# One-core attention and maxout kernel: another written order of the work, the engine of every eviction in that order, another head

## The chip, the cores and the metric

The kernel runs on one core of a Trainium2 chip. The core has a matmul engine (TensorE, PE in the profile, with its weight loads shown as PEld), three engines that calculate on rows of 128 partitions (VectorE is DVE, ScalarE is ACT, GpSimd is POOL), and a queue engine (SyncE, SP). Matmuls write to PSUM, which has eight banks of 128 x 512 numbers in float32; DVE and ACT read the banks and write to SBUF (an eviction). Each engine does its instructions in the order in which the program lists them, and waits where an operand is not there yet. The metric is the device time of one execution in microseconds, median of several runs.

## The reference

The kernel computes two stages one after the other. The first is attention through 32 inducing vectors: `h` is a softmax-weighted mean of each batch's rows of x, and each row of x then takes a softmax-weighted mean of the 32 rows of `h`. The second is a maxout network on each of the 4 x 12544 rows.

```python
x: (4, 12544, 128) float32;  inducing: (32, 128);  w1, w2: (128, 1024);  w_out: (1024, 128)

def mab(q, kv):
    s = scale * (q @ kv.transpose(0, 2, 1))      # scale = 1/sqrt(128)
    s = s - s.max(-1, keepdims=True)
    a = np.exp(s)
    a /= a.sum(-1, keepdims=True) + 1e-09
    return a @ kv
h = mab(I, x)                # I: inducing for each batch; h: (4, 32, 128)
y = mab(x, h)                # (4, 12544, 128)

g = np.maximum(y @ w1, y @ w2)
out = g @ w_out              # (50176, 128) float32
```

## The kernel before, in words

**What it calculates.** max(a, b) is a + relu(b - a), so the network is a linear part through w1 @ w_out and a part relu(y @ (w2 - w1)) @ w_out. With e = exp(scale * x @ h^T), of 32 numbers for each row, y @ (w2 - w1) is e @ (h @ (w2 - w1)) over the sum of e. The relu is taken before the division, which is positive, and the division comes last. The small matrix h @ (w2 - w1) is `hwd`, (32 x 1024), and h @ w1 @ w_out is `m1`, (32 x 128). Both are held four times over, on partitions 0-31, 32-63, 64-95 and 96-127 (quarters q = 0 to 3), so that four matmuls with 32 rows of weights run side by side on PE.

**The pieces.** A batch has 98 chunks of 128 rows. Blocks (28 in all) hold up to four chunks in each of four quarters. One **unit** is 128 x 512 numbers of relu input: four (or two, or one) matmuls with K = 32 into one PSUM bank, then one eviction with relu to SBUF in float16, on ACT (L1102) or DVE (L1105). There are 784 of them. The **final** matmuls (`final_one`, L932, 3136 of them, 128 x 128 x 128) multiply the relus by w_out and accumulate a **group** of up to four chunks in another bank; the linear part is added there by K = 32 matmuls with `m1`; `evict_group` (L964 on DVE, L971 on ACT) multiplies by one over the sum of e and stores 256 KB to DRAM from SP (L989).

**The order by hand.** PE's whole stream is written out in a string `ORDER` of words. A number is that many finals. `pN` is a phase (`phase`, L1031): up to N units of different quarters at once, in PE's row mode (32 x 128 tiles); a quarter that is left out with N below 4 may carry the linear part of a group. `s` is `stage` (L643-670): x @ h^T for a block in column mode (128 x 32 tiles), then exp on ACT. `c`, `t`, `a`, `r`, `e`, `h`, `w`, `m` make the next batch's h: scores (L356), a DMA transpose of their exponentials (`pool_turn`, L395), their product with x (`pool_accum`, L414), and the small steps from it. `xB.J` is a DMA transpose of part J of batch B's x (`transpose_x_dma`, L208) and `gK` the transpose of block K's e (`turn_e2`, L711), after which POOL adds it up and takes reciprocals. Both go to SP's queue, between the stores. PE has three modes in this list: row (`p`), column (`s`, `c`, `a`), and full (the rest). I call a run of words of one mode a segment.

**The planner.** While the list is read, an object `Clock` adds up times of its own for each engine. Its times choose the PSUM bank of each step, and, before the change, the engine of each relu eviction: in `phase` the engine that would be done first takes it, and a number after the point (`p4.13` is 1101 in binary) flips single choices. A string `EVICT` has one digit for each group: 0 for DVE, 1 for ACT.

**The head.** Batch 0 has no h yet. Its x comes in parts of 14 chunks or fewer (`parts[0]`, twelve of them). The first is loaded by SP as float32 and cast by DVE and ACT (L784, L785); the others are loaded by POOL's queue (`load_x`, L195), and the DMA casts from float32 to float16 on the way. The string `HEAD` orders PE there: `3a 3b` transposes the two halves of part 3 on PE (`p1_transpose`, L276; half a is evicted by DVE at L280, half b by ACT at L283), `S3` makes its scores (`p1_scores`, L292) and the exp on ACT (L305), `A3` accumulates h and the sums (`p1_accum`, L319 and L328). Then come the weights: w1 and w2 loaded as float32 by POOL's queue, their difference, the transposes of w1 (`weights_2`, `weights_2b`, L589, L596, L599) and the product w1 @ w_out (`weights_3`, L607, the word `W`). `H` is `second_half`: the second half of `hwd` and the second half of the transposes of w1.

## Time and profile before

| quantity | value |
|---|---|
| time, median of 3 runs | 317.69 us (317.68 to 318.22) |
| the profiled execution's own time | 317.76 us |
| its span in the profile | 316.0 us |
| mean granted clock of PE | 0.998 |
| PE busy | 308.6 us (98%) |
| ACT busy / DVE busy / POOL busy | 280.2 (89%) / 274.5 (87%) / 125.8 us (40%) |
| relu evictions on ACT / on DVE | 470 / 314 |
| mean DMA traffic | 177 GB/s |

The span is what the profiler saw from the first instruction to the last; the execution's own time is 1.76 us more. The page's first part has the busy time of each engine. A matmul's record is longer than the step from it to the next one, since matmuls are pipelined (219 ns on the record of a final, 56 ns from one to the next in the trace), so the busy share of PE does not say how near PE is to its peak. What PE's stream costs is read from the starts of its matmuls. The word list and the trace can be laid side by side: the trace has 151 stretches of row-mode matmuls after the head, and the list has 151 row segments.

### The profile page before, as it was taken

What the parts mean: (1) busy time and instruction counts of PE and PEld (TensorE: products, weight loads), DVE (VectorE), ACT (ScalarE), POOL (GpSimd) and SP (SyncE); (2) the same over time, 40 slices, a digit from 0 to 9 for tenths busy, and PEclk for the clock granted to TensorE, in tenths of its full rate; (3) what the DMA queues carried; (4) which work ended last, traced back from release to release, by engine and by line L of the source; (5) the groups of instructions that cost most, each with busy time, mean ns of one, the idle gap of its engine ahead of it and who ended that gap; (6) DMA issues with size and microseconds to landing.
All of it is one profiled execution on the core that took longest, in us unless ns stands there. A gap on an engine that the chain in (4) does not pass through costs nothing.

```text
span 316.0 us, 12577 instructions
## 1 busy us (share of the span) xinstructions
PE 308.6 (98%) x5308; PEld 239.9 (76%) x5308; DVE 274.5 (87%) x488; ACT 280.2 (89%) x580; POOL 125.8 (40%) x187
## 2 busy tenths in 40 slices
...
GB/s 203 208 252 205 207 219 146 207 229 230 127 218 245 245 183 174 190 233 207 121 225 252 213 227 215 204 174 203 106 85 118 100 106 118 119 88 140 102 120 101
DMA packets 81336, 55.81 MB, mean 177 GB/s; under 512 B 62816, under 2 KB 66176, under 8 KB 81280
## 3 DMA queue, kind: packets, MB, share of 16 engines
...
q0 software_dynamic: 5968, 13.70, 22.4%
...
q14 instruction: 15, 0.12, 0.1%
HBM read 27.28 MB, written 25.69 MB: 168 GB/s over the span
## 4 chain that ended last, share of the span: by engine, by line
PE 94%; DMA 2%; ACT 1%; DVE 1%; issue 1%; POOL 0%; POOLq 0%
PE ps L932 60%; PE ps L1085 23%; DMA xn<-in_x_dram 2%; PE ps L657 2%; PE ps L356 2%; PE ps L414 2%; PE ps L276 1%; PE ps L328 1%; PE ps L292 1%; PE ps L521 0%; DVE relu L1105 0%; PE ps L319 0%; ACT e L669 0%; DVE o L964 0%; ACT e_first L696 0%
## 5 line engine op out<-in xcount | busy, mean ns | idle before, releaser
L1102 ACT ACTIVATE relu<-ps 128x512 f16<-128x512 f32 x470 | 241.0, 627 | 17.5 <-PE ps L1085 16.5
L1105 DVE TENSOR_SCALAR relu<-ps 128x512 f16<-128x512 f32 x314 | 199.7, 684 | 20.6 <-PE ps L1085 19.0
L932 PE MATMUL ps<-woutp,relu 128*128 128x128 f16 x3136 | 203.5, 219 | 0.2
L932 PEld LDWEIGHTS <-relu 128*128 128x128 f16 x3136 | 176.6, 98 | 34.4 <-issue 28.7
L1085 PE MATMUL ps<-e,hwd 32*128 32x512 f16 (+2 forms) x840 | 82.8, 361 | 0.1
L720 POOL TENSOR_TENSOR half<-ed 128x256 f32<-128x256 f16 (+2 forms) x23 | 14.1, 613 | 145.8 <-DMA ed<-e 145.8
L724 POOL TENSOR_TENSOR rd<-den,minus 128x16 f32<-128x16 f32 (+2 forms) x23 | 60.7, 2639 | 1.8
L964 DVE TENSOR_TENSOR o<-ps,rd 128x512 f32<-128x512 f32 (+3 forms) x83 | 53.2, 643 | 3.9 <-PE ps L1085 2.8
L1085 PE MATMUL ps<-m,e 32*128 32x128 f16 x372 | 36.8, 216 | 0.0
L1085 PEld LDWEIGHTS <-hwd 32*128 32x128 f16 x880 | 26.7, 91 | 12.8 <-issue 3.8
L1085 PEld LDWEIGHTS <-e 32*128 32x128 f16 x372 | 22.4, 92 | 10.4 <-issue 2.7
L720 POOL TENSOR_TENSOR half<-half 128x32 f32<-128x32 f32 (+3 forms) x69 | 22.3, 323 | 5.4
L195 POOL DMA_DIRECT2D xn<-in_x_dram x32 | 17.6, 563 | 5.7 <-DMA xn<-in_x_dram 4.3
L280 DVE COPY xT<-ps 128x512 f16<-128x512 f16 (+3 forms) x12 | 5.7, 485 | 8.6 <-PE ps L276 8.6
L964 DVE TENSOR_TENSOR o<-ps,rp 128x512 f32<-128x512 f32 (+3 forms) x20 | 12.8, 642 | 0.0
L369 ACT ACTIVATE eu<-ps 128x512 f16<-128x512 f32 x18 | 11.0, 617 | 0.6 <-PE ps L356 0.3
L669 ACT ACTIVATE e<-ps 128x512 f16<-128x512 f32 (+2 forms) x21 | 11.1, 607 | 0.3 <-PE ps L657 0.2
L283 ACT COPY xT<-ps 128x768 f16<-128x768 f16 (+3 forms) x10 | 5.7, 574 | 4.3 <-PE ps L276 4.2
L276 PE MATMUL ps<-identity,xn 128*128 128x128 f16 x98 | 7.6, 220 | 1.4 <-DMA xn<-in_x_dram 0.9
L657 PE MATMUL ps<-xT,hT 128*32 128x512 f16 (+3 forms) x110 | 8.1, 361 | 0.1
L276 PEld LDWEIGHTS <-xn 128*128 128x128 f16 x98 | 5.5, 97 | 2.9 <-DMA xn<-in_x_dram 1.2
L356 PE MATMUL ps<-xT,inducingT 128*32 128x512 f16 x72 | 6.8, 386 | 0.0
...
## 6 DMA issues: line engine op xcount, KB each, us to landing
...
xT<-xn SPq DMA_TRANSPOSE x33, 4.4
...
```

Of the source, the lines that this page charges most:

```text
L195: nc.gpsimd.dma_start(out=xn_at[b, i][:, 0:n, :], in_=xr[b, :, k0 : k0 + n, :])
L276: nc.tensor.transpose(ps[:, j, :], xn[:, g + j, :], identity16)
L356: nc.tensor.matmul(out=ps[32 * g : 32 * (g + 1), :], lhsT=inducingT, rhs=xT_tiles[b % 2][:, U * u + 4 * g : U * u + 4 * (g + 1), :], start ...
L657: nc.tensor.matmul(out=ps[32 * q : 32 * (q + 1), 128 * t : 128 * (t + n)], lhsT=hq, rhs=xT[:, c : c + n, :], start=True, stop=True, tile_p ...
L669: nc.scalar.activation(out=blk.e2[:, 0 : 128 * wd], in_=ps[:, 0 : 128 * wd], func=AF.Exp, scale=st[0]["rs"] if blk.b == 0 else scale,)
L720: nc.gpsimd.tensor_tensor(out=dst, in0=cur[:, :, 0:n], in1=cur[:, :, n : 2 * n], op=ALU.add)
L724: nc.gpsimd.tensor_tensor(out=rp[:, 0:wd, :].rearrange("p t q -> p (t q)"), in0=den[:, 0 : 4 * wd], in1=minus1[:, 0 : 4 * wd], op=ALU.pow,)
L932: nc.tensor.matmul(out=g.ps[:, 128 * c : 128 * (c + 1)], lhsT=g.blk.relu[g.q][:, 128 * (jb * w4 + t) : 128 * (jb * w4 + t + 1)], rhs=woutp ...
L964: nc.vector.tensor_mul(osb[:, 0:m, :], g.ps[:, 0 : m * C].rearrange("p (s c) -> p s c", s=m), g.blk.rp[:, t0 : t0 + m, q : q + 1].broadcas ...
L1085: nc.tensor.matmul(**seq.pop(0))
L1102: nc.scalar.activation(out=dst, in_=src, func=AF.Relu)
L1105: nc.vector.tensor_scalar(out=dst, in0=src, scalar1=0.0, scalar2=None, op0=ALU.max)
```

## The change

- **Head.** Batch 0 is cut into thirteen parts instead of twelve. Six of them (2 to 7, 56 chunks) are now loaded by POOL's queue as float32 without a cast, into slots of the relu buffers that are still free (`homes`, `wide`). A word `C` in `HEAD` (`cast_x`) then casts one of them: the first half on DVE, the second half on POOL, after which POOL issues the next load. Eight loads are issued at the start and the others one after each cast, or at the word `L`. `x` after a transpose word swaps its eviction between DVE and ACT. The sums of the exponentials are padded to four chunks, and the two parts of two chunks share one. The three small operations on the identity (`diag`, `rep32`, `repd`) are ahead of the first cast on DVE. The second difference of the weights is on POOL instead of DVE, the second cast of w1 on POOL instead of ACT, and all eight transposes of w1 are in one word `V` after `H`.
- **List.** `ORDER` is another list, with the same 3136 finals, 27 stages, 18 scores and 33 transposes of x. The number after the point of a `p` is now the engine of each eviction itself (bit set: DVE). `EVICT` has six groups on ACT instead of five, the last three among them. The words `x` stand elsewhere, behind the times that the planner has for the landing of their loads.
- **Buffers and planner.** PSUM is one tile with eight slices, the relu buffers and the output buffers are fixed slices of tiles instead of buffers of a pool; their number is the same. The planner's constants are others. A way to split a final in four (`narrow`) is in the code, and no word of the list uses it.

```diff
-    PAIR = 0.0558
-    SWITCH = {"full": 0.11, "row": 0.097, "col": 0.097}
+    PAIR = 0.0563
+    SWITCH = {
+        "full": {"row": 0.095, "col": 0.095},
+        "row": {"full": 0.082, "col": 0.088},
+        "col": {"full": 0.1, "row": 0.094},
+    }
...
+    psall = psum.tile([128, 8, 512], F32, name="psall", tag="psall")
+    relus = [big.tile([128, 2, 4096], F16, name=f"relus{q}", tag=f"relus{q}") for q in range(4)]
...
-    parts[0] = [(0, 14), (14, 14), (28, 14), (42, 14), (56, 7), (63, 7), (70, 7), (77, 7), (84, 6), (90, 4), (94, 2), (96, 2)]
+    parts[0] = [(0, 14), (14, 7), (21, 7), (28, 14), (42, 14), (56, 7), (63, 7), (70, 7), (77, 7), (84, 6), (90, 4)]
+    parts[0] += [(94, 2), (96, 2)]
...
+        homes = {0: (2, 0, 0, 14), 2: (0, 1, 0, 7), 3: (1, 1, 0, 14), 4: (2, 1, 0, 14)}
+        homes.update({5: (0, 1, 7, 7), 6: (3, 1, 0, 7), 7: (3, 1, 7, 7)})
...
+        def load_next():
+            dst, src = later.pop(0)
+            nc.gpsimd.dma_start(out=dst, in_=src)
+
+        load_next()
+        make_identity(nc, identity16)
+        load_next()
+        make_identity(nc, identity32)
+        for _ in range(6):
+            load_next()
...
+        def cut(n):
+            h = min(8, (n + 2) // 2)
+            return (0, h), (h, n - h)
+
+        def cast_x(i):
+
+            for half, (g, m) in enumerate(cut(parts[0][i][1])):
+                eng = nc.gpsimd if half else nc.vector
+                eng.tensor_copy(out=xn_at[0, i][:, g : g + m, :], in_=wide[i][:, g : g + m, :])
...
+            load_next()
...
         HEAD = """
-        1a 1b I S0 2a 2b S1 A0 S2 3a 3b A1 4a 4b S3 S4 A2 A3 5a 5b A4 6a 6b S5 7a 7b S6 A5 8a 8b S7
-        A6 9a 9b 10a S8 11a N S9 S10 A7 S11 A8 A9 A10 A11
+        1a 1b 0b C2 I 2b 2a S0 C3 S1 C4 S2 A0 A2 C5 3b A1 3ax 4a 4b S3 5b C6 5a 6a S4 C7 A3 S5 6b A4 L
+        7ax 7bx S6 A5 8bx 8a 9a 9b S7 A6 10bx 10a 11ax S9 12a N S8 S10 A7 S11 S12 A9 A8 A10 A11 A12
         """
...
-        for i in range(7):
-            if i == 3:
-                difference(nc.gpsimd, 512, J, 22.4, 1.2)
+        load_x(1, 0)
+        difference(nc.vector, 0, 256, 20.45, 0.34)
+        difference(nc.gpsimd, 256, 512, 20.45, 0.64)
+        load_x(1, 1)
+        load_x(1, 2)
+        difference(nc.gpsimd, 512, J, 22.35, 1.25)
+        cast_w1(1)
+        for i in range(3, 7):
             load_x(1, i)
-        difference(nc.vector, 0, 256, 21.0, 0.3)
         sums = small_h(0)
-        difference(nc.vector, 256, 512, 21.0, 0.3)
-        weights_2(0)
...
-                if (max(ck.act, ready) + 0.477 <= max(ck.dve, ready) + 0.597) != bool(flip >> k & 1):
-                    nc.scalar.activation(out=dst, in_=src, func=AF.Relu)
...
+                relu_out(q, blk, unit, bi, ready, bool(vector >> k & 1))
...
         ORDER = """
-        s p4.13 s H1 W g2 p4.1 p2 8 m0 4 p3 p2.1 10 p3 p2 13 p3.2 6 p4.5 22 p2 p4.8 17 x1.0 p4.8 4 g1 11
-        p4.1 13 p4.9 p1 16 p3.4 p2 14 p4.10 6 x1.1 4 x1.2 x1.3 x1.4 x1.5 x1.6 2 p3.6 s s s s 6 g3 6 p4.5
-        14 x1.7 1 x1.8 p4.8 19 p4.10 p2.1 12 x1.9 5 p3 14 p4.4 c1.0 15 p1 p4.5 14 p4.3 g4 13 p4.8 25 p4.6
-        p3.2 10 x1.10 17 p2 p3.1 15 c1.1 p4.2 12 t1.1 2 p3 6 p4.2 4 g5 11 c1.2 c1.3 p4.1 18 p4.4 t1.3 21
-        p3.5 p3 22 c1.4 p1.1 p4.1 19 p2 p4.8 5 g6 21 p4.2 p2 c1.5 19 r1 a1.1 p3.2 p4 t1.5 19 a1.3 p4.9
-        p2.2 29 p3.3 p4 26 p4.1 a1.5 5 p3.1 p2.3 1 e1 11 p4.12 1 h1 17 w1 s s s s p3.2 19 m1 15 p4.6 p3.6
-        30 p3.1 p3.3 24 p3 p3.3 27 p3.2 p3.1 20 p4.3 p2 15 s p4.1 18 p2.1 p3 15 g7 g8 7 p3.3 p4.2 9 g9 12
-        x2.0 3 x2.1 x2.2 s p1.1 p4.4 x2.3 12 p4.5 14 p4.6 14 p4 14 p3 21 p3.6 p4.8 14 g10 4 x2.4 4 x2.5
-        x2.6 9 p4.13 s c2.0 14 p4.6 p1 5 x2.7 4 x2.8 13 p3.3 p3.4 23 p4.4 11 c2.1 p4 p1 9 t2.1 4 g11 x2.9
-        4 x2.10 10 p4.3 p3 15 c2.2 p3.3 21 p3.1 p3.5 27 p3.3 p3.2 c2.3 19 p4.10 4 g12 4 t2.3 5 p4.1 17
-        p3.1 p3.4 16 a2.1 c2.4 p3.1 p3.1 23 p4.4 18 p2.1 p4.9 13 g13 17 p4.9 p3.3 24 a2.3 c2.5 p4.1 p2 7
-        t2.5 12 r2 18 p3 p4.2 30 p4.10 p2.2 16 a2.5 p4.3 p3.6 8 e2 10 p4.2 2 h2 21 p3.1 p3.6 11 w2 4 m2
-        15 p4.11 s s s 13 p3 p2 12 s p4 15 p2 p3.2 22 p3.5 p3.2 3 x3.0 4 x3.1 19 p3.4 p4.12 25 p3.3 13 p3
-        p3.3 27 p3.2 p3.5 12 g15 8 g14 3 p4 11 s s p3.1 p2.2 14 x3.2 4 x3.3 4 x3.4 x3.5 5 p3.1 p4.5 19
-        x3.6 17 p3.4 p4.1 23 g16 14 p4.4 p3 27 c3.0 s p3.1 15 x3.7 c3.1 p4.2 p1 x3.8 15 p4.4 21 p3.4 p3 8
-        g17 14 p3.3 p2 6 t3.1 12 p4.2 p1 20 p3.4 p3.4 22 p4.10 p2.1 30 p4.3 p3 4 g18 8 x3.9 4 x3.10 7
-        c3.2 a3.1 c3.3 p4.3 p2 9 t3.3 15 p4.4 17 p2.1 p4.8 27 p2.2 p4.1 13 g19 18 p3.3 p4.4 10 r3 8 c3.4
-        c3.5 a3.3 p4.5 20 t3.5 1 p4.8 p2.2 21 p4.4 13 p3.5 p2 1 g20 27 p4.4 p3.3 27 a3.5 p4.8 p2.3 2 e3
-        16 h3 14 p3.5 p4.2 10 w3 4 m3 15 s p4.1 9 g21 10 p3.1 p2.1 15 p3.5 s s s 13 p3.1 p3.4 22 p4.8 p1
-        27 p4.3 p3 9 g22 13 p2.2 p2 22 p3.2 p4.3 25 s s p3.4 13 p3 p3.3 30 p4.9 p3.2 g23 21 p4.2 20 p4.1
-        p2.2 30 p3.4 p4.2 24 s p2 p3.2 12 p4.8 g24 22 p4.6 p2.2 20 p2.1 p3.2 16 p3.1 p2 11 p4.9 21 p4.3 9
-        p1 p3 g25 p1 20 p3.1 p3.4 30 p4.8 p3.1 26 p4.8 13 p4.6 13 p4.3 9 g26 13 p3.3 p3 27 p3.5 p2 22 p2
-        p4.1 22 p2.2 p4.9 22 p3 p2.1 g27 27 p4.1 p3.2 38 p4.3 p3.1 31 p2 p4.9 22 p2.1 p3.1 24 p3 p4.11 40
-        p3.4 p3 21 p4.6 21 p2.1 p3.4 31 p4.4 p4.3 63
+        s p3.2 p3.3 s H1 V W p3.4 p3.4 8 m0 5 g2 3 p3.2 4 p3.4 9 p3.6 7 p4.2 12 p3.1 10 p4.5 8 p3.2 10
+        p4.4 x1.0 21 p4.3 p1 10 p4.10 x1.1 23 p2.1 p4.1 23 x1.2 x1.3 p3.2 9 p4.13 s s s 18 p1 p4.5 x1.4
+        14 p4.1 4 g3 13 p4.12 9 p3.1 3 x1.5 8 p4.12 15 c1.0 x1.6 p3.3 p2 16 p4.1 10 x1.7 6 x1.8 5 p4.3
+        p2.1 14 s c1.1 p3.4 6 x1.9 g4 8 p4.9 15 p4.6 8 p3.4 20 p2.1 p4.1 22 p4.10 11 p1 p4.12 3 x1.10 14
+        c1.2 c1.3 p4.9 21 g5 p4.1 t1.1 p2.1 t1.3 27 p4.12 p2 21 p4.10 20 p4.12 p2 23 p4.12 a1.1 c1.4 a1.3
+        c1.5 p3.2 11 r1 t1.5 14 p4.12 p3.1 31 p3.4 g6 p3.1 10 a1.5 p4.2 4 e1 16 h1 6 p4.9 p3.4 18 w1 9 s
+        s p4.9 25 p3.1 p3.4 33 p4.12 p3 23 m1 3 p3.4 16 p2.2 p4.4 20 p1.1 p3.1 16 p4.9 8 s s p3.2 2 x2.0
+        14 p2.2 p4.4 21 p4.5 22 p3.2 g9 p3.4 9 x2.1 14 x2.2 p4.12 6 x2.3 13 x2.4 p4.8 p2.1 5 x2.5 23 p2.2
+        p4.8 23 x2.6 x2.7 p2.1 p3.4 12 p4.4 16 p4.12 11 p3.5 g10 c2.0 c2.1 15 x2.8 p1 p4.12 14 p4.8 17
+        p4.6 13 p3.6 s x2.9 t2.1 s c2.2 15 p4.5 10 p3.2 p2.2 x2.10 14 g11 p4.4 15 p4.3 15 c2.3 p2.3 p4 27
+        p2.2 p4.2 31 p4.1 p3.3 28 p4.3 t2.3 10 g12 c2.4 g8 a2.1 c2.5 p3.2 p3.2 28 p2.1 t2.5 p4.8 23 p4.12
+        10 s a2.3 p2.2 p4.4 28 p4.8 p2.2 1 g13 r2 13 a2.5 p3.4 5 p4.2 8 e2 6 p4.8 24 p3.2 p3.1 10 h2 20
+        p4.8 p2.1 12 w2 5 m2 6 p3.5 s s s 10 p4.9 22 p4.12 p2.1 18 p4.1 15 p3.4 13 p3.2 6 p4.5 7 x3.0 7
+        p4.12 9 s p3.6 21 p4.8 p2.2 19 g15 12 x3.1 x3.2 p4.1 p3.1 30 p2.2 p4.8 31 x3.3 p3 p4.12 29 p4.10
+        11 p3.1 g16 12 c3.0 p4.12 18 x3.4 x3.5 3 p4.2 p3.4 4 x3.6 26 p3.6 p3 20 p3.7 x3.7 s x3.8 s c3.1
+        12 p4.1 14 g17 t3.1 p4.12 21 p3.2 p4.10 19 x3.9 7 p2.1 p3.4 24 p3.4 p3.4 23 p4.12 x3.10 18 p2.1
+        g18 p4.8 14 p3.5 c3.2 a3.1 s c3.3 13 p3.4 p3.2 23 p4.10 6 p3.2 12 g1 p4.12 t3.3 21 p2.2 p4.2 7 r3
+        27 g19 p3.1 p4.6 28 p4.6 c3.4 a3.3 c3.5 10 p4.5 p2 12 t3.5 21 p3.2 p4.12 31 p3.4 p3.2 23 g20 g7
+        p4.2 a3.5 p1 p3.4 11 e3 2 p4.2 12 h3 11 p3.4 p3.5 7 w3 8 s s s p3.2 8 m3 13 p1 g21 p4.1 23 p3.6
+        p2 16 p4.8 15 p3.3 8 p4.2 27 p3.3 p4.2 23 p3.4 17 g22 6 p4.10 p3.1 39 p3.6 p3 31 p3.1 p4.5 31
+        p2.2 p4.2 11 g23 p3.2 17 p4.5 15 p4.14 s s s 20 p3.2 p3.4 26 s p4.3 12 p3.4 6 g24 p4.2 22 p2.1
+        p4.8 21 p4.12 12 p1 p4.5 14 p4.6 21 p2 p4.9 20 g25 5 p3.2 3 p4.6 17 p4.3 19 p4.8 p2.2 31 p3.6
+        p4.8 g14 31 p2.1 p4.3 12 g26 p3.2 21 p2.1 p4.4 32 p4.7 p3 32 p2 p4.6 32 p3.4 p4.3 31 g27 p2.1
+        p4.2 28 p4.1 p2.1 24 p4.1 p2.1 31 p3.2 p3.6 28 p2 p4.12 25 p2 p3.1 36 p3.1 p4.1 51
         """
 
-        EVICT = "000000000000000000000000101000000000000000000000010000000000000000000010000000000000000000000000000000010000"
+        EVICT = "000000000000000000000000000000000000000000000000000100000000000000000000000001000000000000000000000010000111"
```

293 lines of the change are left out of this document (168 added, 125 removed).

## The prediction

> **What bounds the kernel now.** I read the page first: its busy shares, the costliest groups and the chain that ended last.
>
> ```profile
> span 316.0 us, 12577 instructions
> PE 308.6 (98%) x5308; PEld 239.9 (76%) x5308; DVE 274.5 (87%) x488; ACT 280.2 (89%) x580; POOL 125.8 (40%) x187
> PE 94%; DMA 2%; ACT 1%; DVE 1%; issue 1%; POOL 0%; POOLq 0%
> L1102 ACT ACTIVATE relu<-ps 128x512 f16<-128x512 f32 x470 | 241.0, 627 | 17.5 <-PE ps L1085 16.5
> L1105 DVE TENSOR_SCALAR relu<-ps 128x512 f16<-128x512 f32 x314 | 199.7, 684 | 20.6 <-PE ps L1085 19.0
> L932 PE MATMUL ps<-woutp,relu 128*128 128x128 f16 x3136 | 203.5, 219 | 0.2
> L1085 PE MATMUL ps<-e,hwd 32*128 32x512 f16 (+2 forms) x840 | 82.8, 361 | 0.1
> ```
>
> The chain is PE for 94% of the span, and PE's two great groups have 0.2 and 0.1 us of idle time before them, while both evicting engines lose some 17 to 21 us waiting for PE. So PE's own stream is the time, from about 30 us on. The busy times by stretch and the chain's start say where that is not so.
>
> ```profile
> 0.00:23.00 23.00, 20.00 (x352) 15.26 (x353) 9.81 (x32) 12.46 (x27) 12.50 (x29) 1.00 1.03 222
> 23.00:31.00 8.00, 6.72 (x107) 4.58 (x106) 7.16 (x16) 7.44 (x17) 3.36 (x5) 1.00 1.06 203
> 31.00:97.00 66.00, 66.00 (x1136) 50.17 (x1134) 60.02 (x105) 62.97 (x132) 26.31 (x38) 1.00 1.02 200
> 104.00:300.00 196.00, 195.98 (x3380) 153.66 (x3378) 179.76 (x308) 181.60 (x375) 83.61 (x116) 1.00 0.71 166
> ```
>
> (Columns: PE, weight loads, DVE, ACT, POOL, granted clock, DMA share, GB/s.) In the head the DMA share is 1.03: loads set the pace. From 23 to 31 us PE stands idle 1.3 us, and ACT is at 93%:
>
> ```profile
> 24.50 0.49 ACT relu L1102
> 24.99 0.58 ACT e L669
> 25.56 0.48 ACT w1s L599
> 26.09 0.40 PE ps L607 x4
> ```
>
> That is the word W: its second four matmuls wait for the second half of w1's transposes, which ACT evicts behind a relu and an exp. What is left in the body is small and local, as here, where a row segment that elsewhere ends after 0.54 us ends after 0.97 (97.31 to 98.28):
>
> ```profile
> 97.31 0.39 PE L1085 MATMUL ps<-e,hwd 32*128 32x512 f16 x3
> 97.43 0.92 PE L1085 MATMUL ps<-e,hwd 32*128 32x512 f16 x4
> 98.28 1.29 PE L932 MATMUL ps<-woutp,relu 128*128 128x128 f16 x20
> ```
>
> **The sum** starts from the profiled execution, 317.76 us (span 316.0 and 1.76 around it), 0.07 above the median of the three runs.
>
> **Head, loads.** In the packet records of the trace each of the 16 DMA engines takes 8 rows of every part. A row with a cast takes 288 ns for 14 chunks, 154 for 7, and 135, 98 and 60 for 6, 4 and 2; rows without one take 159 ns for 4096 bytes (weights) and 121 for 3072 (part 0). Before: 3 x 8 x 288 + 4 x 8 x 154 + 8 x (135 + 98 + 60 + 60) = 14.66 us, and the records run from 4.57 to 19.32 us, so this sum is the pace. After: two parts of 14 uncast, 8 x (159 + 121) each, four of 7 at 8 x 140, two of 7 with a cast, and the same small ones: 14.24. The last part lands 0.42 us sooner. The bytes by time say the same less sharply: uncast weights come at 382 to 434 GB/s, cast x at 208 written, so 416 read; over the 3.67 MB that change kind this bounds the shift from -0.4 to +0.8.
>
> **Head, PE behind the last landing.** Before, from the end of the last transpose (19.84) to the end of the accumulations (21.6):
>
> ```profile
> 19.69 0.29 PE L276 MATMUL ps<-identity,xn 128*128 128x128 f16 x2
> 20.18 0.33 PE L328 MATMUL ps<-et,xn 128*128 128x32 f16 x7
> 20.64 0.32 PE L328 MATMUL ps<-et,xn 128*128 128x32 f16 x6
> 21.41 0.22 PE L328 MATMUL ps<-head,xn 128*128 128x32 f16 x2
> ```
>
> With their sums an accumulation costs 0.32 us for 7 chunks, 0.38 for 6, 0.2 for 4. The old list has S9 S10 A7 S11 A8 to A11 there, 1.72 us; the new one also S8, a part of 7 more, and one sum less: 1.99. So 0.27 of the 0.42 is given back: -0.15. The small steps behind are unchanged; the four transposes of w1 that leave them (0.23 us) lay beside the wait for the sums. DVE's six half casts (0.70 us for 8 chunks by its cast of part 0, half that for 4, 2.9 in all) lie in the 8.6 us that it waits for PE there.
>
> **Head, POOL.** This chain is new: half a cast and a load issue (0.55 us, row L195), six times, and PE's words 5b, 6b, 7b wait for it. POOL's cast is in no row. Bounds: its memset (543 ns for 512 columns, 220 for 128) gives 0.75 us for 768 columns, its two-input adds (1269 ns for 512, 457 for 128) 1.8. I take 1.3, the middle, since a cast reads one operand, and 0.7 for 384. From landings at 9.6, 11.6, 12.6, 13.6 and 15.7 (the packet sum) POOL ends part 7 at 16.65. PE then has 2.35 us of work to the last transpose and is there at 19.0, before its data at 19.25: no cost, with 0.25 to spare. At 1.8 it ends at 18.4 and PE is 1.45 late.
>
> The Trainium skill's page SBUF — State Buffer, section "SBUF: two separate sides", says that a DVE copy in a two-port mode and a POOL instruction hold a shared port pair exclusively, one fully waiting for the other. Here both halves of a cast start together. The trace half agrees: the one POOL issue beside DVE's float32 cast (4.67 us) took 655 ns instead of 535 to 557, 0.11 more where a full wait would be 0.5. By the rule the sum would be 0.7 us higher; it is rival C.
>
> **Start of the body.** The new list has six evictions instead of four before W, and ACT has the chain: e_first to 23.41, exp 0.59, three relus at 0.49, exp 0.58, w1's transposes 0.48. W's end moves from 26.43 to 27.05. For that one phase more is done (0.21 us), and the wait of 0.29 us for the first relu (27.40 to 27.70) goes, since two more units are done: +0.62 - 0.21 - 0.29 = +0.12. ACT's cast of w1 (0.62) is now POOL's and ends near 24.7, just before its reader. Both ends: -0.3 if ACT catches up, +0.7 if the waits add.
>
> **The list, counted.** Durations are medians of the old list's segments in the trace, start to next start. A row segment of one phase takes 0.327 us, of two 0.541 to 0.584, of three 0.68. The old list has 53, 97 and 1, the new one 85, 79 and 0: 72.07 against 71.49 us, -0.58. Leaving full mode costs 0.096 us (152 ns from final to phase, less 56): 150 times before, 161 after, +1.06. Leaving column mode costs about 0.098: 33 against 26, -0.68. Together -0.20. Finals, stages and scores are the same in number.
>
> **Waits in the body.** The old row segments sum to 74.90 us, 2.83 above their medians; 1.3 of that lies in waits over 60 ns, which come where two evictions queue on one engine ahead of a bank that PE wants (97.5, 102.8, 234 us). The new list has its own waits, and no row of before shows them. Bounds: none left, -2.8, or twice as many, +2.8. Nearest are the segments by kind: one-phase ones lie 0.01 us above their minimum, two-phase ones 0.04, so 32 more of the first and 18 less of the second give -0.4; and evictions fixed in the list (307 on DVE at most, 477 on ACT) load both as before: 250 us at 0.604 and 261 at 0.488, with the rest, in 287. I take -0.9: two thirds of the large waits go.
>
> **DMA transposes.** Moved `x` and `t` words stand in SP's queue between stores; behind them wait the stores and the six output buffers. A store held there is covered by those buffers (DVE waited 0.4 us in all for one). The tightest new place is t1.5: 4.4 us of PE work before a1.5 where it had 6.5. It issued 1.6 us after its place, and such a transpose lands in 3.1 to 4.9 (median 3.5). I take 0, as the next word's work can be short by its own waits; bound +2.1.
>
> **The end.** The last three groups go to ACT: 376 ns for 128 columns against DVE's 281, and two behind each other in 0.62 against 0.41. The last store leaves later: +0.15 (0 to 0.3).
>
> Sum: 317.76 - 0.15 + 0.12 - 0.20 - 0.9 + 0.15 = **316.8 us**.
>
> **The rivals.**
> - A, the waits stay: the new list queues as much as the old. For it: the loads of ACT and DVE are equal; against: fewer two-phase segments. 317.7.
> - B, slower, POOL's casts: they cost what its two-input adds cost. PE is 1.45 late at the last transpose, and the weights, issued behind, too. It decides from 0.25 us of delay in POOL's chain on. For it: the nearest arithmetic rows; against: one operand. 318.2 with the large waits gone, 319.1 with them; 318.7.
> - C, turns of DVE and POOL: each cast waits for the other engine's, so POOL ends part 7 at 17.6 instead of 16.65; 0.7 later, 317.5. Against: the 0.11 above.
> - D, slower, a1.5 waits for its transpose by the bound: 318.9; with c3.1 (5.2 us behind x3.4, where landings take 4.4 plus the queue) alike. Against: no such wait in the profile.
>
> **How the numbers follow.** Forecast 0.50 (its own range 315.6 to 317.05), A 0.20, B 0.15, C 0.07, D 0.08. Faster by over 0.2% (0.64 us, about what can be told from no change) is the forecast, 0.50; same is A and C, 0.27; slower B and D, 0.23. The range, 315.6 to 318.7, goes from most of the large waits gone to the middle of B; outside lie half of B and D and a little below.
>
> **What would show it.** Right: the last L276 transpose before 19.4 us, row segments in sum near 73.5 us, PE idle after W about as before, no idle PE from 31 us on. Wrong: POOL casts over 1.5 us and PE waiting for them at 16 to 18 us (B); a DVE cast that starts late beside a POOL one (C); PE waiting for a DMA at L414 or L356 (D); segments as long above their medians as before (A).

## The result and the profile after

The changed kernel took 319.14 us (median of 16 runs, 317.96 to 323.21), the kernel before 317.75 beside it (16 runs). The ratio is 1.0035, with a 95% interval of 1.0019 to 1.0051, so it is slower by about a third of a per cent. Two of its 16 runs, 323.0 and 323.2 us, lie over 1.5% above its fastest and are left out of the ratio. The forecast was 316.8, and its range ended at 318.7. The profiled execution of the changed kernel took 318.53 us with a span of 316.8: 0.8 more than the profiled one before.

The page of the changed kernel: span, engines, the shares in the chain, the groups of relus, finals and units, and the scores of the later batches (L411).

```profile
span 316.8 us, 12594 instructions
PE 306.8 (97%) x5306; PEld 239.7 (76%) x5306; DVE 274.4 (87%) x489; ACT 282.8 (89%) x587; POOL 132.5 (42%) x196
...
PE 89%; DMA 4%; DVE 1%; POOL 1%; SPq 1%; ACT 1%; issue 1%; ACTq 0%; POOLq 0%
...
L1110 ACT ACTIVATE relus<-psall 128x512 f16<-128x512 f32 x473 | 241.3, 626 | 17.5 <-PE psall L1170 17.1
...
L995 PE MATMUL psall<-woutp,relus 128*128 128x128 f16 x3104 | 203.9, 220 | 0.0
...
L1170 PE MATMUL psall<-e,hwd 32*128 32x512 f16 (+2 forms) x840 | 80.9, 362 | 0.0
...
L411 PE MATMUL psall<-xT,inducingT 128*32 128x512 f16 x72 | 7.7, 384 | 1.4 <-DMA xT<-xn 1.4
```

PE's share of the chain fell from 94% to 89%, and DMA's rose from 2% to 4%. The last line says where: the scores of a later batch (L411, the word `c`) waited 1.4 us for the DMA transposes of x. The windows of the forecast, for the changed kernel (PE, weight loads, DVE, ACT, POOL, granted clock, DMA share, GB/s):

```profile
0.00:23.00 23.00, 19.71 (x347) 14.27 (x347) 12.54 (x41) 12.71 (x29) 18.34 (x36) 1.00 0.98 295
23.00:31.00 8.00, 6.51 (x105) 4.34 (x104) 6.21 (x14) 7.17 (x16) 4.40 (x7) 1.00 1.11 199
31.00:97.00 66.00, 66.00 (x1151) 51.02 (x1147) 61.62 (x107) 62.76 (x132) 26.23 (x38) 1.00 0.95 188
104.00:300.00 196.00, 194.04 (x3346) 153.03 (x3339) 178.43 (x302) 180.75 (x373) 79.27 (x111) 1.00 0.75 170
```

From 31 to 97 us PE is full as before. Behind 104 PE is idle for 1.96 us where it was full before (195.98). PE's timeline at the words `c2.0 c2.1`, with each wait in brackets:

```profile
118.77 0.40 PE L411 MATMUL psall<-xT,inducingT 128*32 128x512 f16 x3
119.53 0.39 PE L411 MATMUL psall<-xT,inducingT 128*32 128x512 f16 x2 [0.37 <-DMA xT<-xn]
120.34 0.39 PE L411 MATMUL psall<-xT,inducingT 128*32 128x512 f16 x2 [0.41 <-DMA xT<-xn]
121.37 0.38 PE L411 MATMUL psall<-xT,inducingT 128*32 128x512 f16 x1 [0.64 <-DMA xT<-xn]
```

By the starts of the matmuls these three gaps are 1.92 us longer than the usual step. Why x was late stands in POOL's timeline. First the kernel before, then the changed one (`...` marks a line left out):

```profile
84.34 0.18 POOL L194 COPY pace<-hacc 128x1 f32<-128x1 f32 x1 [2.18 <-DVE hacc L447]
84.84 3.81 POOL L195 DMA_DIRECT2D xn<-in_x_dram  x7 [0.31 <-PE ps L932]
```

```profile
87.45 0.43 POOL L774 TENSOR_TENSOR half<-ed 128x128 f32<-128x128 f16 x1 [10.39 <-DMA ed<-e]
87.96 0.94 POOL L774 TENSOR_TENSOR half<-half 128x64 f32<-128x64 f32 x3
...
89.26 1.65 POOL L778 TENSOR_TENSOR rd<-den,minus 128x8 f32<-128x8 f32 x1
90.86 0.18 POOL L213 COPY pace<-hacc 128x1 f32<-128x1 f32 x1
90.99 1.18 POOL L214 DMA_DIRECT2D xn<-in_x_dram  x2
```

The copy `pace` and the seven loads of batch 2 stand behind the word `a1.5` in POOL's queue. The new list has `g6` just ahead of `a1.5`. `g6` asks for the transpose of block 6's e, and POOL then adds that block up: it waits for the transpose and works 3.4 us, and only then can it issue the loads, 6.15 us later than before. The last of the seven landed at 113.47 instead of 106.96.

The new list also asks for the transposes of x sooner. The first, `x2.0`, was issued on SP at 101.85, when its own load had landed (97.25) but others were still in flight:

```profile
101.85 5.30 SPq L227 DMA_TRANSPOSE xT<-xn  x1
```

It landed at 114.50, 1.0 us behind the last load. Before, it was issued at 108.30, behind all loads, and landed 3.7 us later. The others followed, and PE's three gaps end with the landings of `x2.2` to `x2.4` (119.49, 120.30 and 121.33). In the traces here the first transpose of a batch, when it is issued among that batch's loads, lands 0.7 to 2.6 us behind the last of them; why is not shown.

### The profile page after: what moved, and what is told of

Its sections match the earlier page's. It is cut to its first block, busy times and chain, and to the rows that moved or that the text cites. A ratio compares the mean times of both kernels' runs of the same rounds, so it can differ in the third digit from the quotient of the medians.

```text
span 316.8 us, 12594 instructions
## 1 busy us (share of the span) xinstructions
PE 306.8 (97%) x5306; PEld 239.7 (76%) x5306; DVE 274.4 (87%) x489; ACT 282.8 (89%) x587; POOL 132.5 (42%) x196
## 3 DMA queue, kind: packets, MB, share of 16 engines
HBM read 27.28 MB, written 25.69 MB: 167 GB/s over the span
## 4 chain that ended last, share of the span: by engine, by line
PE 89%; DMA 4%; DVE 1%; POOL 1%; SPq 1%; ACT 1%; issue 1%; ACTq 0%; POOLq 0%
PE psall L995 59%; PE psall L1170 22%; DMA relus<-in_x_dram 3%; PE psall L710 2%; PE psall L411 1%; PE psall L470 1%; SPq L227 1%; DMA xT<-xn 1%; DVE relus L1107 1%; POOL relus L280 1%; PE psall L318 1%; ACT relus L1110 1%; PE psall L578 1%; PE psall L383 0%; PE psall L334 0%
## 5 line engine op out<-in xcount | busy, mean ns | idle before, releaser
L1110 ACT ACTIVATE relus<-psall 128x512 f16<-128x512 f32 x473 | 241.3, 626 | 17.5 <-PE psall L1170 17.1
L1107 DVE TENSOR_SCALAR relus<-psall 128x512 f16<-128x512 f32 x303 | 194.0, 685 | 20.0 <-PE psall L1170 18.3
L995 PE MATMUL psall<-woutp,relus 128*128 128x128 f16 x3104 | 203.9, 220 | 0.0
L995 PEld LDWEIGHTS <-relus 128*128 128x128 f16 x3104 | 174.9, 98 | 34.3 <-issue 28.9
L1170 PE MATMUL psall<-e,hwd 32*128 32x512 f16 (+2 forms) x840 | 80.9, 362 | 0.0
L1030 DVE TENSOR_TENSOR osbs<-psall,rd 128x512 f32<-128x512 f32 (+1 forms) x82 | 53.4, 651 | 2.7 <-PE psall L1170 1.3
L1170 PE MATMUL psall<-m,e 32*128 32x128 f16 x372 | 36.8, 217 | 0.0
L1030 DVE TENSOR_TENSOR osbs<-psall,rp 128x512 f32<-128x512 f32 (+3 forms) x20 | 12.9, 645 | 2.4 <-PE psall L995 2.2
L425 ACT ACTIVATE eu<-psall 128x512 f16<-128x512 f32 x18 | 10.9, 612 | 1.4 <-PE psall L411 1.4
L723 ACT ACTIVATE e<-psall 128x512 f16<-128x512 f32 (+2 forms) x21 | 10.8, 581 | 0.1
L318 PE MATMUL psall<-identity,xn 128*128 128x128 f16 x98 | 8.4, 228 | 1.8 <-POOL xn L307 1.2
L318 PEld LDWEIGHTS <-xn 128*128 128x128 f16 x98 | 6.0, 101 | 4.3 <-POOL xn L307 1.9
L411 PE MATMUL psall<-xT,inducingT 128*32 128x512 f16 x72 | 7.7, 384 | 1.4 <-DMA xT<-xn 1.4
```

The costliest lines, as they stand in the source:

```text
L318: nc.tensor.transpose(ps[:, j, :], xn[:, g + j, :], identity16)
L411: nc.tensor.matmul(out=ps[32 * g : 32 * (g + 1), :], lhsT=inducingT, rhs=xT_tiles[b % 2][:, U * u + 4 * g : U * u + 4 * (g + 1), :], start ...
L425: nc.scalar.activation(out=eu, in_=ps, func=AF.Exp, scale=scale, accum_out=st[b]["es"][:, u : u + 1])
L995: nc.tensor.matmul(out=g.ps[lo:hi, 128 * c : 128 * (c + 1)], lhsT=relu[:, lo:hi], rhs=woutp[:, jb, :], start=not g.started, stop=(state["m ...
L1030: nc.vector.tensor_mul(osb[:, 0:m, :], g.ps[:, 0 : m * C].rearrange("p (s c) -> p s c", s=m), g.blk.rp[:, t0 : t0 + m, q : q + 1].broadcas ...
L1107: nc.vector.tensor_scalar(out=dst, in0=src, scalar1=0.0, scalar2=None, op0=ALU.max)
```

## The experiments

Times are medians; "beside" is the kernel before, run on the same chip. A wait in the text is counted from start to start, less the usual step, and is up to 0.2 us a gap longer than the idle time in the brackets. The mean granted clock of a run is 1.00, or 0.995, 0.989, 0.984 and so on; what the steps mean comes below. It was under 0.997 in 1 of 113 such runs of the kernel before. "At full clock" means a mean of 1.00.

### The late loads: e1, e3, e19

e1 is the changed kernel with one word of the list moved:

```diff
- ... t1.1 p2.1 t1.3 27 p4.12 p2 21 ... p3.4 g6 p3.1 10 a1.5 p4.2 ...
+ ... t1.1 p2.1 t1.3 27 g6 p4.12 p2 21 ... p3.4 p3.1 10 a1.5 p4.2 ...
```

> The changed kernel with one word moved: g6 (the transpose of block 6's e, whose sum POOL makes) stands behind t1.3 and its 27 finals, some 8 us sooner, instead of 10 finals ahead of a1.5. Theory (POOL's queue): the loads of batch 2, which POOL issues after a1.5, no longer stand behind g6's sum; they are issued near 85 us instead of 90.99, PE's waits at c2.0 and c2.1 for the transposes of x (1.9 us in the profile of the changed kernel) go, and the median falls by 1.5 to 2.5 us, to 316.7 to 317.6. Rival (SP's queue or the place of c2.0 and c2.1): the loads come sooner, but PE still waits over 1 us at the scores of batch 2, and the median stays within 0.7 us of the changed kernel's.

It took 317.10 us (316.51 to 318.46, 12 runs; beside 318.16), ratio 0.9976 (0.9961 to 0.9990): 2.0 below the changed kernel, and faster than before. POOL's loads go out at 85.58 by its timeline:

```profile
85.09 0.18 POOL L213 COPY pace<-hacc 128x1 f32<-128x1 f32 x1 [4.00 <-DVE hacc L504]
85.58 3.82 POOL L214 DMA_DIRECT2D xn<-in_x_dram  x7 [0.31 <-PE psall L995]
```

and by PE's the eight matmuls of batch 2's first two scores run without a gap:

```profile
119.24 0.62 PE L411 MATMUL psall<-xT,inducingT 128*32 128x512 f16 x8
```

e3 does the reverse to the kernel before, and nothing else:

```diff
- ... p2 p4.8 5 g6 21 p4.2 ... p4 26 p4.1 a1.5 5 ...
+ ... p2 p4.8 5 21 p4.2 ... p4 16 g6 10 p4.1 a1.5 5 ...
```

> The kernel before with the one word g6 moved to where the new list has it, some 10 finals ahead of a1.5. Theory (POOL's queue): its loads of batch 2 are then issued some 5 to 6 us later, near 90 us, and PE waits for DMA transposes at the scores or the first stage of batch 2: 0.5 to 2.5 us slower than before, with more spread between runs. Rival: the old list's places for x2 and c2 have room for it, or the lateness is not from this word: within 0.3 us of before.

It took 321.20 us (6 runs; beside 318.16), ratio 1.0095 (1.0074 to 1.0117). POOL issued the loads at 91.71, and PE stood at the same scores:

```profile
119.13 0.39 PE L356 MATMUL ps<-xT,inducingT 128*32 128x512 f16 x2 [1.46 <-DMA xT<-xn]
```

e19, at the end, puts `g6` back to its late place in the best kernel (e17, below).

> e17 with g6 put back to where the change has it, just ahead of a1.5. The loads of batch 2 leave POOL some 6 us later and PE waits for their transposes at c2.0 and c2.1: 1.9 us by the changed kernel's profile, 2.0 by the first run, and up to 1.2 more where a half-clock stretch follows: 316.8 to 318.1. Rival: the first run's gain came from elsewhere (another bank or eviction order that the move of g6 brought), 314.9.

317.74 us (11 runs) against e17's 314.91: 2.83 more, of which the profile shows 1.23 as waits at `c2`. All three agree: the place of this one word is worth 2 to 3 us, more than the whole result. At full clock the differences are 1.8 (changed kernel against e1), 2.3 (e3 against the kernel before) and 2.3 (e19 against e17). What is more goes with the granted clock, taken up below: in e3's profile it is 0.50 from 120.24 to 123.66 us, right behind the wait. Of e19's 2.3 us the waits at `c2` are about half; the other half is not placed.

### Which part holds the rest: e4, e5

e4 is the changed kernel with the old loads and the old word order of `HEAD`; e5 has the new head with the old list, every eviction on the engine that it had before.

> The changed kernel with the old head's loads: twelve parts, all but the first cast by their DMA, all issued at the start, the old order of HEAD; the list, the evictions, the weights' steps and the buffers are the new ones. If the uncast loads and the casts on DVE and POOL gave what I forecast (0.15 us), this is 0.2 us slower than the changed kernel; if they cost time (the last x landed 0.3 us later than before in the profile), it is 0.2 to 0.6 us faster. A difference over 1 us either way would mean that the head decides the result.

318.21 us (12 runs; beside 318.16), ratio 1.0018 (0.9995 to 1.0041). It waits 1.24 us at `c2` and 1.48 at `W`. It is 0.9 below the changed kernel, with intervals that overlap.

> The changed kernel with the old list: every phase, word and group as before, each relu eviction on the engine that it had before, w1's transposes in one word behind H. If the list (with g6 late) makes the result, this is near the time of before, 317.5 to 318.3, with little spread; its row segments sum to 74 to 75 us again. If the head or the fixed buffers make it, it is at 319 or more.

320.45 us (6 runs; beside 318.16), ratio 1.0069 (1.0051 to 1.0087). Neither expectation had this: without the new list and without the late loads, still 2.3 us above before. Laid beside the kernel before by row segments, e5 is 0.14 us late at the first one, 1.48 at the second (27.90 against 26.42) and 2.10 at the third (30.41 against 28.31); after that it stays so within 0.7. The second step is W's wait, 1.27 us. The third had no wait at all, but a granted clock of 0.50 from 26.76 to 30.17 us, and another such stretch from 13.10 to 16.51. So the clock has to be looked at.

### Waits that only give way to others: e6, e7, e8

e6 is e1 with `r2` (the last scores of batch 2 and their exp on ACT) moved forward, since `a2.5` waits for that exp:

```profile
151.52 0.24 PE L489 MATMUL psall<-xn,et 128*32 128x128 f16 x2 [0.54 <-ACT et L445]
```

```diff
- ... p2.2 p4.4 28 p4.8 p2.2 1 g13 r2 13 a2.5 ...
+ ... p2.2 p4.4 28 r2 p4.8 p2.2 1 g13 13 a2.5 ...
```

> The changed kernel with two words of its list moved: g6 as in the first run (behind the 27 finals after t1.3), and r2 (the scraps' scores of batch 2 and their exp on ACT) from 13 finals ahead of a2.5 to ahead of the p4.8 before. Theory: PE's 0.70 us wait for ACT's exp in a2.5 (150.76 in the first run's profile) goes whole, as it stands on PE's own stream with no slack behind it: 0.7 below the first run's 317.1, so 316.4 (316.1 to 316.7). Rival: the wait covers one that comes due next (the landing of t2.5's turned tile, or the exp's queue on ACT further ahead), and the time stays at 317.1.

317.55 us (12 runs; beside 318.21): nothing gained. The wait is gone and the rival is right, with a wait that it named only in general: batch 3's scores now come early for their x, whose loads stand behind `g13` in POOL's queue as batch 2's stood behind `g6`:

```profile
186.64 0.38 PE L411 MATMUL psall<-xT,inducingT 128*32 128x512 f16 x1 [0.33 <-DMA xT<-xn]
```

e7 issues POOL's difference and cast of the weights ahead of two loads of batch 1, and e8 turns w1 ahead of the first relus as well. The edit of e7:

```diff
-        load_x(1, 1)
-        load_x(1, 2)
         difference(nc.gpsimd, 512, J, 22.35, 1.25)
         cast_w1(1)
-        for i in range(3, 7):
+        for i in range(1, 7):
             load_x(1, i)
```

> The kernel of e6, with POOL's difference of the weights' second half and its cast of w1 issued ahead of the loads of batch 1's parts 1 and 2 (1.11 us of POOL's queue). H's 0.57 us wait for that difference goes. Theory: nothing is gained, since the word W behind it waits for DVE, whose copy of the turned w1 stands behind three relus and hwd (24.27 to 26.73 in the first run) whether H is early or not; W's wait grows from 1.14 to about 1.7 and the time stays at e6's, 316.4. Rival: H's wait is a cost by itself, 0.5 below e6, 315.9.

317.60 us (12 runs; beside 318.21), as the theory said, no gain. e8 has the cast ahead of the difference, the difference of columns 256 to 512 on DVE, and in the list:

```diff
- s p3.2 p3.3 s H1 V W p3.4 ...
+ s V p3.2 p3.3 s H1 W p3.4 ...
```

> The kernel of e6, with w1's transposes (word V) moved from behind H to behind the first s, ahead of the six evictions of p3.2 p3.3; for that POOL casts w1's second half first, DVE takes the difference of columns 256 to 512 (as in the kernel before), and POOL's difference of the second half comes ahead of the loads of batch 1's parts 1 to 6. Theory: the start of the body is bound by the two copies of turned w1 behind those relus and by H; with both ahead, W has nothing to wait for (1.14) and H little (0 to 0.3 of the 0.57), while the relus come 0.42 (DVE) and 0.58 (ACT) later, which later waits may take back in part: 0.5 to 1.2 below e6, 315.2 to 315.9. Rival: the relus set the start (PE waits for the first finals instead), time as e6, 316.4 or above.

317.72 us (12 runs): a miss. W still starts at 27.26, and the profile names what it waited for, the load of w_out:

```profile
27.26 0.62 PE L660 MATMUL psall<-woutp,relus 128*128 128x128 f16 x8 [1.62 <-DMA woutp<-in_moe_w_out_dram]
```

That load was issued at 19.33 and landed at 27.21; in e1, issued at 19.37, it landed at 24.96. Why it took 2.3 us more is open, so e8 does not test what it was made for.

### The granted clock

The page of e5 shows a lower digit in the row of the clock. In fifteen stretches, in the profiles of eleven of the kernels run here, PE's granted clock is 0.50: twelve last 3.41 us, two 6.83 and one 13.66. Where one profile has two, their starts lie 13.66 (e5), 10.24 (e6), 13.65 (e7) and 27.31 us (e15) apart, which are 4, 3, 4 and 8 times 3.41. So a grid of 3.41 us runs beside the program, with another offset in each run. All but one begin behind 3.41 us in which PE's records cover 51 to 76%, which is 0.8 to 1.7 us of idle time (the first of e15 begins behind a span with no matmul at all). Other spans of the grid at 56 to 85% are not followed by one, so the exact measure stays open. One stretch of 3.41 us is 0.005 of a run's mean clock, which is how the steps 0.995, 0.989, 0.984 are to be read.

The Trainium skill, page "TensorE: Matmul & The Clock Gate", section "What's actually happening", describes this: PE's clock drops to half after an idle window of 3413 ns on a free-running count. Grid, length and ratio agree with the runs. The rule of thumb in the page's section "HAM oscillation — how this bites in real kernels", no idle gaps over 3.4 us, does not: here stretches began behind windows whose longest single gap was 0.5 to 1.6 us.

The new head thins PE's work out. The windows from 8 to 14 us, before and then changed:

```profile
8.00:10.00 2.00, 1.47 (x30) 1.25 (x28) 1.44 (x5) 1.13 (x2) 0.40 (x1) 1.00 1.09 217
10.00:12.00 2.00, 2.00 (x61) 1.93 (x58) 0.69 (x1) 1.43 (x3) 0.53 (x1) 1.00 1.05 203
12.00:14.00 2.00, 2.00 (x50) 1.97 (x48) 0.84 (x2) 1.37 (x3) 1.07 (x2) 1.00 1.14 209
```

```profile
8.00:10.00 2.00, 1.34 (x35) 1.23 (x35) 0.76 (x3) 1.55 (x3) 1.09 (x2) 1.00 1.00 412
10.00:12.00 2.00, 1.39 (x40) 1.22 (x37) 0.69 (x1) 0.64 (x3) 1.82 (x2) 1.00 1.05 437
12.00:14.00 2.00, 1.65 (x32) 1.31 (x30) 1.27 (x3) 1.71 (x2) 1.68 (x2) 1.00 1.00 416
```

PE is idle for 1.62 of these 6 us instead of 0.53. The profiled execution of the changed kernel had no stretch; 12 of its 16 runs had one or more, by their mean clock, and two of them (0.984 and 0.982) three or more.

### The head by itself: e9, e10, e13, e15, e18

e9 is e1 with the old loads and the old word order of the head; e10 has the old steps of the weights as well (differences and copies as before, only the second four transposes of w1 behind `H`).

> The first run's kernel (g6 early) with the loads and the order of the head as before: all of x's parts cast by their loads, the old words of the head; list, weights' steps and buffers as changed. It prices the new head without the waits for batch 2. If the head gains what the prediction summed (0.15), this is 0.15 above the first run, 317.25; if it costs what the last landing shows in the profile (19.62 against 19.32 us), 0.3 below, 316.8; if the old loads make the weights later at the body's start, as W's wait in e4 says (1.48 against 1.14), 317.4 to 317.6. All three lie close; beyond 0.5 us either way something else in the head counts.

316.16 us (315.63 to 316.55, 5 runs, all at a clock of 1.00; beside 318.21), ratio 0.9937 (0.9925 to 0.9949): 0.9 below e1, where no expectation had more than 0.3. The clock explains little of it: e1's two runs at full clock took 316.91 and 317.06 us, still 0.8 above e9. What else the new head costs over the old is not settled; that x and the weights land later in it, as e13 and e18 show, is one candidate.

> The kernel of e9 (new list with g6 early, old loads and old order of the head) with the steps of the weights as before too: the differences of columns 0 to 512 and the first copy of turned w1 on DVE ahead of the body, w1's second half cast by ACT, only the second four transposes of w1 behind H. Of the change the list, its eviction engines and the fixed buffers are left. Theory: PE's waits at H and W (1.74 us at 25.00 in e9, 1.14 in before at 24.90) shrink by about 0.5, as DVE's copy no longer stands behind three relus and hwd: 315.6 (315.2 to 315.9). Rival: the six relus ahead of W on both engines set W's time whichever way w1 comes: as e9, 316.2.

317.38 us (12 runs; beside 317.97), ratio 0.9975. Four runs at a clock of 1.00 took 316.0 to 316.2, as e9; six with one stretch 316.9 to 318.8. So at full clock the steps of the weights are worth nothing; but 8 of e10's 12 runs had a stretch and none of e9's five. W's wait (1.81 us in e10) was not shortened: ACT's copy stands behind the three relus in both. One stretch at the body's start costs 1.4 us.

e13 tries to keep the clock up in the new head:

```diff
- 1a 1b 0b C2 I 2b 2a S0 C3 S1 C4 S2 A0 A2 C5 3b A1 3ax 4a 4b ...
+ 1a 1b 0b C2 I F2 2b 2a S0 C3 S1 C4 S2 A0 A2 C5 F2 3b A1 F2 3ax F1 4a F1 4b ...
```

(`Fn` is n matmuls of the warm-up kind.)

> The first run's kernel (new head, g6 early) with six added matmuls of the warm-up kind (512 columns, result unused) in the head where PE stands idle: two behind I, two ahead of 3b, one ahead of 3a's other half-tile, one ahead of 4a and 4b's halves. In the first run's profile the granted clock is 0.50 from 10.86 to 14.28 us, behind 3.41 us in which PE was busy for 67%. Theory: the half clock follows a stretch with too little PE work; with it filled the clock stays at 1.00 in the head, the mean clock of the runs is 1.000 in most (first run: 0.993 to 0.995 in nine of twelve, 1.000 in two), and the time is 316.9 in the median with a narrower spread. Rival: the half clock comes from elsewhere (the denser loads, all engines busy at once): mean clocks as in the first run, and the fillers add up to 0.3, 317.4.

317.84 us (12 runs; beside 317.97). The clock stayed at 1.00 in 8 of 12 runs instead of 2, so the theory of the idle time holds; but the time rose by 0.7, more than either said (eight matmuls were added, not the six of the text). Its eight runs at full clock still have a median of 317.6 us, so the half clock is not the main cost of the new head. In its profile x lands late besides (a wait of 1.49 us at 15.21). It is no remedy.

e15 issues every load ahead of the casts: `while later: load_next()` at the start, and no `load_next()` in `cast_x`.

> The first run's kernel (new head, g6 early) with all loads of x and the weights issued ahead of POOL's casts, as in the kernel before, instead of one behind each cast; casts and sizes as changed. Theory (the weights land late because their loads are issued behind casts, and DVE's difference, which stands ahead of hT, waits for them): DVE's wait at L625 goes, the median falls to e9's 316.2 (up to 316.6). Rival (uncast loads and casts on chip are slower as such): as the first run, 317.1.

328.81 us (6 runs; beside 318.24): both wrong. POOL's load issues wait for earlier loads to land, and the casts now stand behind them, in POOL's timeline and then in PE's:

```profile
10.58 0.53 POOL L280 DMA_DIRECT2D xn<-in_x_dram  x1 [1.85 <-DMA relus<-in_x_dram]
...
18.89 4.83 POOL L307 CAST xn<-relus 128x384 f16<-128x384 f32 x6
```

```profile
19.46 0.93 PE L317 MATMUL psall<-identity,xn 128*128 128x128 f16 x7 [11.71 <-POOL xn L307]
```

The clock was at half for 13.66 us. POOL's one queue for loads and arithmetic is the same trap as with `g6`.

e18 gives the price of the new head as a whole: e17 (next section) with only the new loads, casts and word order of `HEAD` put back.

> e17 with the changed kernel's loads and head instead of those before (parts 0 and 2 to 7 uncast, cast by DVE and POOL, each next load issued behind a cast); weights' steps, list, W's place and the added zeros as in e17 (314.91). By the prediction's step for the head 0.15 below e17, 314.75; by e1 against e9 some 0.9 above, 315.8, with mean clocks of 0.995 in most runs from PE's idle time at 8 to 14 us. If the half clock is all of it, the runs with a mean clock of 1.00 lie at 314.9.

317.17 us (11 runs, none at a clock of 1.00; beside 318.06) against 314.91: **2.3 us more**, half clock and later landings together. The windows of its profile show the order of things: thin work, then half clock, then PE full but late.

```profile
10.00:12.00 2.00, 1.04 (x34) 0.84 (x29) 0.69 (x1) 0.71 (x3) 1.28 (x1) 1.00 1.04 427
12.00:14.00 2.00, 1.58 (x27) 1.42 (x28) 0.74 (x2) 1.34 (x2) 1.66 (x3) 0.89 0.99 412
14.00:16.00 2.00, 2.00 (x32) 2.00 (x31) 1.75 (x3) 1.07 (x2) 2.00 (x5) 0.50 1.06 305
```

The last transpose of x starts at 20.80 there (e17: 19.72), and the first `s` of the body at 24.11 (22.60). Part of this is the weights: DVE's difference stands ahead of hT, and waits for their landing 0.19 us in the changed kernel, 0.65 in e18, 1.15 in e6, and in e7

```profile
23.54 0.42 DVE L625 TENSOR_TENSOR w<-relus 128x256 f16<-128x256 f32 x1 [1.62 <-DMA relus<-in_moe_w_dram]
```

The weights land at 21.36 in the changed kernel and at 23.51 in e7. Of these 2.15 us, 0.65 come from loads issued later (18.06 against 17.41); but in e18, issued at 17.41 too, they landed at 22.43. That rest is open.

### The clock at W, and the best kernel: e11, e12, e14, e16, e17

e11 is e10 with `r2` early; e12 also has `g13` behind `a2.5` and the last three digits of `EVICT` as 000.

> e10 with r2 ahead of p4.8, as in e6, in a kernel whose head leaves the clock alone. The 0.70 us wait in a2.5 goes: 0.7 below e10, 314.9 if e10 is 315.6. Rival: another wait takes its place, as e10.

317.26 us (11 runs; beside 317.97). At a clock of 1.00 it takes 315.7 to 316.5, only 0.2 below e10: waits of 0.80 us for x in batch 3 take the place of the 0.70, as in e6.

> e11 with g13 behind a2.5 (the loads of batch 3 come 1 to 3 us sooner) and the last three groups' evictions on DVE instead of ACT. By the prediction's term for the end (+0.15 on ACT) 0.15 below e11; the loads of batch 3 have cover, so nothing from g13: 314.75. Rival: the end is set by the last store alone, as e11, within 0.1.

316.12 us (6 runs), ratio 0.9945 (0.9925 to 0.9965); 315.14 and 315.15 at a clock of 1.00, 0.7 below e11. The waits in batch 3 are gone, so `g13` did count, and from the last matmul's start to the end of the span it is 3.21 us instead of 3.48.

e14 fills W's wait with zeros:

```diff
             for jb in range(NJB):
+                if jb == 4:
+                    for _ in range(24):
+                        nc.tensor.matmul(out=ps[:, 0:128], lhsT=warm[:, 0:128], rhs=warm[:, 0:128], start=False, stop=False)
                 nc.tensor.matmul(
```

> e12 with 24 added matmuls of 128 columns of zeros into W's own accumulation (they add nothing), between W's first four and second four, where PE stands idle for 1.81 us. They take 24 x 0.056 = 1.34 us of that idle time. Theory (the half clock of 3.41 us follows a stretch with too much idle time, here at W): the mean clock of the runs is 1.00 in nearly all (e12: 0.995 in three of six, 0.989 in one), and the median falls from 316.1 to e12's undisturbed 315.15. Rival (something else lowers the clock): clocks and median as e12.

315.13 us (314.82 to 315.45, 4 runs, all at a clock of 1.00; beside 318.24), ratio 0.9899: e12's time at full clock in every run, with added work; without the zeros four of e12's six runs had a stretch. This is the cleanest test of the clock. The windows at the start of the body, first e10, then e14:

```profile
24.00:26.00 2.00, 0.93 (x9) 0.58 (x9) 1.97 (x4) 2.00 (x5) 2.00 (x4) 1.00 1.10 216
26.00:28.00 2.00, 1.25 (x17) 0.83 (x17) 0.06 (x1) 0.99 (x4) 0.07 (x1) 0.58 1.04 203
28.00:30.00 2.00, 2.00 (x24) 1.75 (x21) 1.68 (x4) 2.00 (x4) 0.00 (x0) 0.50 1.06 208
```

```profile
24.00:26.00 2.00, 1.83 (x29) 1.67 (x30) 1.97 (x4) 2.00 (x5) 2.00 (x5) 1.00 1.07 214
26.00:28.00 2.00, 1.70 (x34) 1.19 (x31) 0.49 (x1) 1.41 (x4) 0.14 (x1) 1.00 1.07 210
28.00:30.00 2.00, 1.98 (x34) 1.41 (x30) 1.57 (x5) 2.00 (x6) 0.00 (x0) 1.00 1.05 208
```

In the last window e10 fits 24 matmuls where e14 fits 34. e16 is e12 with `W` behind the first `p3.4` (`V p3.4 W p3.4`), and e17 is e16 with 8 matmuls of zeros in W.

> e12 with W behind the first p3.4 instead of ahead of it. That row segment (0.55 us) needs only hwd, done at 25.97 in e12, and W's second four matmuls start at 26.75 there, behind ACT's copy. Theory: the segment fills part of W's wait, which falls from 1.81 to about 1.2: 0.5 below e12 (half-clock stretches aside), and fewer of those: median 315.2 (best runs 314.6). Rival: hwd's copy and the banks hold the segment as long as W: as e12, 316.1.

315.85 us (6 runs), ratio 0.9916; the one run at a clock of 1.00 took 314.53. The wait moved to hwd's copy and was not over, so five of six runs had a stretch.

> e16 with 8 added matmuls of zeros (0.45 us) between W's two halves. Theory: no half-clock stretches left (mean clock 1.00), median at e16's best, 314.6 (314.4 to 314.9). Rival: the added matmuls stand on the path, up to 0.45 above e16.

**314.91 us** (314.83 to 315.04, 4 runs, all at 1.00; beside 318.24), ratio 0.9893 (0.9870 to 0.9916). It beats both kernels. It has the new list with its evictions, but for four words moved (`g6`, `r2`, `g13`, `W`) and the last three groups back on DVE, the old head with the old steps of the weights, and zeros against the half clock.

## Why the prediction was wrong

The failed step is **"DMA transposes ... I take 0"**. It looked at what `x` and `t` words meet in SP's queue and left the moved `g` words out of account, though a `g` word puts 3.4 us of POOL's work, and a wait, ahead of the next batch's loads. It cost 1.92 us in the profile, 2.0 by e1 and 2.8 by e19 (2.3 at full clock). The bound of +2.1 had the size by accident, and for another place. Rival D foresaw a wait for transposes and a time of 318.9, near the result, but at `a1.5` and `c3.1` and by stores on SP; there PE did not wait. That its time came near is chance. The list of what would show the forecast wrong did hold L356, the scores, which are L411 in the changed kernel and did wait.

Point by point, with the sum's own terms:

- **Head, loads (-0.42 landing).** Wrong. The last part of x landed 0.30 later (19.62 against 19.32). In the packet records a 14-chunk row without a cast (7168 bytes) takes 272 ns against 288 with one. The sum had costed it as 159 + 121 ns from the rows of weights and part 0, 280 ns; that was near. By the records x's packets add up to 14.23 us after the change, as forecast, yet they take 15.10 us (4.53 to 19.63); before, 14.63 took 14.75. So the sum of packet times is not the pace. From 6.5 to 11 us the share is 1.07 before, at 213 GB/s written, so 426 read, and 1.02 after, at 424 GB/s. So the records overlap more with a cast, both kinds read x at the same rate, and by this there was nothing to gain. The forecast's second bound, by bytes (-0.4 to +0.8), holds what was measured.
- **Head, POOL ("no cost, with 0.25 to spare").** The casts took what was assumed, 1.35 us for 768 columns (1.3 forecast) and 0.52 to 0.76 for 384 (0.7), but by luck: alone they take 0.83 and 0.52, and the rest is a wait for DVE's cast (below, rival C). POOL ended part 7 at 17.46, not 16.65, mainly since the load of part 7 landed at 16.65, not 15.7. PE waited 1.2 us in all for POOL's casts at L318. In the profiled run, which had no half clock, the body's first `s` starts 0.07 sooner all the same. Over the runs the new head costs 0.9 (e1 against e9, 0.8 at full clock) to 2.3 us (e18 against e17, with the half clock that its idle time brings), and the part that is not the clock stays open.
- **Start of the body (+0.12).** Too low. W ended at 27.28, not 27.05, since H waited 0.50 us for POOL's difference and W for DVE, whose copy stands behind three relus and hwd. At 34 us the changed kernel has five finals and six row-mode matmuls (two of units, four of the linear part) more to do, about 0.45 us.

```profile
24.80 0.38 PE L578 MATMUL psall<-w,hT 128*128 128x512 f16 x1 [0.50 <-POOL w L625]
...
26.73 0.62 PE L660 MATMUL psall<-woutp,relus 128*128 128x128 f16 x8 [0.97 <-DVE relus L648]
```

- **List (-0.20) and waits in the body (-0.9).** Right in sign and too small. The row segments sum to 71.69 us (74.90 before, about 73.5 forecast), with the changes of mode as counted (+1.06, -0.68): -2.83 instead of -1.1. Nearly all waits in row segments went, not two thirds of the large ones.
- **A wait not looked for**: `r2` stands 13 finals ahead of `a2.5`, and ACT's exp comes 0.70 us late (152.65 us).
- **The end (+0.15).** Right: from the last matmul's start to the end of the span 3.41 us against 3.28; kernels with these groups on DVE have 3.17 to 3.22.

By the profile: 317.76 + 0.45 - 2.83 + 1.92 + 0.70 + 0.15 = 318.15, against 318.53; some 0.4 is not placed. The median lies 0.6 above that profiled run. Twelve of 16 runs had half-clock stretches, which that run had not, but they are not the whole reason: the other three runs at full clock took 318.63, 318.97 and 320.33 us, and the fastest of all, 317.96, had a stretch. That part stays open.

The rivals: A's waits went. B's cast prices did not come. C's turns did come, at less than its price. In four of the changed kernel's six pairs of casts DVE's half starts 0.03 us before POOL's, as here:

```profile
12.29 0.69 DVE L307 CAST xn<-relus 128x1024 f16<-128x1024 f32 x1 [1.46 <-DMA relus<-in_x_dram]
12.32 1.35 POOL L307 CAST xn<-relus 128x768 f16<-128x768 f32 x1 [0.33 <-DMA relus<-in_x_dram]
```

DVE's takes 0.69 us, and POOL's 1.35 where one with no DVE instruction beside it took 0.83 (e15, at 19.34); for 384 columns it is 0.76 beside a cast of DVE and 0.52 without. In e15, where POOL's casts often came first, DVE's took up to 1.45 us for 1024 columns and 1.63 for 512, instead of 0.69 and 0.43. So one waits for the other, whichever is second. The rule of the Trainium skill, page "SBUF — State Buffer", section "SBUF: two separate sides", is that the two exclude each other in full; these casts agree with it. The load issue that the prediction held against C is no such test. POOL's end of part 7, 17.46, lies near C's 17.6, but mostly by the late load: the turns were in the prices of 1.3 and 0.7 already.
